# W's mirrored rows by indirect DMA, x in eight pieces, two more pairs' sums on TensorE, and a new order of items, in a two-layer spectral and dense kernel

## The chip, the cores and the metric

The kernel runs on one core of a Trainium2 chip. A core has a matmul engine (TensorE, PE in the profile, with PEld for its weight loads), a vector engine (VectorE, DVE), an activation engine (ScalarE, ACT), a general engine (GpSimd, POOL) and a queue engine (SyncE, SP) that issues most DMAs; ACT and POOL can issue DMAs too. Each engine runs its own list of instructions in order, and the engines wait for each other through semaphores. The metric is the device time of one execution in microseconds (us): lower is better.

## The reference

Two layers, each a spectral filter (A) and a dense block (B), both on a layer-normalised x of 2048 x 448 in bf16, with the same weights in both layers.

```
def _A_ref(x, w_r, w_i):                   # x: (1, 2048, 448)
    X = rfft2(x.astype(float32))           # 2048 x 225
    X = X * (w_r + 1j * w_i)
    return irfft2(X, s=(S, D)).astype(bfloat16)

def _B_ref(x, w1, b1, w2, b2):             # w1: 448 x 1792, w2: 1792 x 448
    h = x @ w1 + b1
    r = where(h > 0, h, 0)
    return (r * r) @ w2 + b2

x = x + _A_ref(_layernorm(x)); x = x + _B_ref(_layernorm(x))
x = x + _A_ref(_layernorm(x)); x = x + _B_ref(_layernorm(x))
```

## The kernel before

The transforms are matmuls with constant matrices. The 2048 rows are split as 16 x 128. Partition p of `xin` holds rows 16p to 16p + 15, so that tile t is row 16p + t of every partition.

- **First transform (A1)**, for each of 16 tiles: statistics of the layer norm (on DVE; on ACT for tiles 1, 3 and 5, `act_stats`, L835), a root on ACT and a reciprocal on DVE, then `first_A` (L859). It scales the 128 x 256 matrix `FA_sb` by the tile's 1/std into `Fs`, on POOL, ACT or DVE, and runs five matmuls of 256 columns with `xin`, with `xr` (the mirrored half of the columns, made by eight copies "XR" of two tiles each) and with the mean. The result is copied from PSUM to `XA`.
- **Transform along D (TD)**, for each of eight pairs p of the 16 components (pair 0 holds components 0 and 8): `stage_TD` (L916), result in `U`.
- **B**: `stage_B` (L933), the transform over the remaining 128 positions by `G_sb`, result in `EF`. A pair's two results E and F are those of the real and of the imaginary component.
- **W**: `stage_W` (L966), on DVE. It forms E - F and E + F with parts exchanged (L978, L979), except where TensorE has made the sums (`V_PAIRS`, in layer 2), then four products with W and four to eight sums, into `Z`. It is called for pair 1, pairs 2 and 3, pairs 4 and 5, pairs 6 and 7, and pair 0.
- **Bi** (`stage_Bi`, L1005), the inverse over the 128 positions, by `H_sb` or `HS_sb`, into `VT`; then `stage_TI` and `stage_AI`, which complete the inverse for tiles of rows and add x; then the second norm and the dense block: `h_part`, `h_pairs`, `o_tile`. `w1_aux` (L784) makes column sums of w1 for the folded norm, 16 matmuls with a block of ones; three DMAs write them to a row block of `W1_sb`.

W has a row for each of 2048 frequencies. Pair p needs rows 16k + p and, mirrored over k, rows 16(127 - k) + 16 - p. Before, the second kind is loaded as it stands into `Wn`, which shares memory with `yT`, and `w_mirror` (L802) turns its partitions round: two matmuls of 224 columns with the exchange matrix `J_sb`, and a copy from PSUM to `Wt`. `Wt` is 32 rows of 224 elements to a partition; `Wp` and `W08` are views of it.

The order of the work is fixed: every instruction (or group on one PSUM tile) is an item with a number, and `ORDER` lists the numbers for each engine. The scheduler (`_Sched.schedule`, L347) takes the head of each list, gives out the eight PSUM banks, and fills gaps of PE that it foresees with matmuls of a block of ones (L1338). A tile's waits are worked out from what it reads and writes. The DMA lists are part of `ORDER`: SP issues its DMAs in the order of its list, and an issue that has to wait holds up all behind it.

Of the kernel before, what the change touches and what calls it, by code (L numbers as in the profile page):

```python
# [6 lines left out]
ALU = mybir.AluOpType  # L7
BF16 = mybir.dt.bfloat16
FP32 = mybir.dt.float32

# [14 lines left out]
V_PAIRS = (1, 2, 3, 4, 5, 6, 7)  # L25
H_PAIRS = tuple(p for p in range(1, 8) if p not in SD_PAIRS)
# [10 lines left out]
def make_constants():  # L37
# [64 lines left out]
    for g, M in enumerate((cl * np.cos(th), cl * np.sin(th))):  # L102
        for r in range(2):
# [4 lines left out]
    return dict(HS=HS, FA=np.concatenate([FA, -FA], 1), FI=np.concatenate([FI, -FI], 1), TD=TD, G=G, H=H, TI=TI, TQ=TQ,  # L108
                J=np.eye(P)[::-1])
# [17 lines left out]
1332 1373 1382 1387 1392 1397 1402 1407 1412 1420 1423 1417 1426 1429""",  # L127
# [142 lines left out]
class _Sched:  # L270

    ENGINES = ("pe", "act", "dve", "pool", "sp")
    NDSEM = {"sp": 20, "pool": 16, "act": 8, "pe": 0, "dve": 0}
    DMA_RATE = 400.0
    TURN = 100.0
    BEGIN = 800.0
    WINDOW = 3413.0  # L280

    def __init__(self):
        self.ops = {e: [] for e in self.ENGINES}
# [1133 lines left out]
```

## Time and profile before

| | |
|---|---|
| time, median of 3 runs | 271.43 us (271.36 to 272.04) |
| the profiled execution's own time | 271.52 us |
| its span, first to last instruction | 269.7 us |
| PE busy | 261.0 us, 97% |
| DVE / ACT / POOL busy | 206.1 / 178.9 / 11.9 us |
| DMA | 16.71 MB, of which 10.85 MB read from HBM and 1.84 MB written |
| granted TensorE clock | 0.999 |

The span is what the profile sees; the time holds some 1.8 us more around it. The profile's slices cut the span in 40 parts of 6.74 us, and a digit is the busy tenths of a slice. A line of the timeline has the start in us, the duration (of a merged run of instructions, from the first start to the last end), the engine, the line of the kernel, the operation, out<-in, and in brackets the idle time before it and what ended it. A line of groups has the count, the busy time and the mean of one in ns, then the idle time before. Matmul ends are modelled; the steps from start to start are what PE took.

### The profile page before, as it was taken

The page shows a single profiled execution, that of the slowest core. Times are in us where ns is not written, and L with a number is a line of the kernel's source. Part 1 is how long each engine was busy: PE and PEld are TensorE (multiplying, and loading weights), DVE is VectorE, ACT ScalarE, POOL GpSimd, SP SyncE. Part 2 cuts the span into 40 slices and gives each one's busy share as a digit, 9 for nine tenths or more (in the row PEclk, how much of TensorE's full clock was granted, in tenths as well). Part 3 has the DMA queues.
Part 4 walks back from the last instruction along what each step waited for, and adds up shares of the span by engine and source line. Part 5 has one row for each costly group of instructions (what it writes and reads, how often), then busy time and mean ns, then how long its engine had stood idle before and what let it go on. Part 6 is the DMA issues. An engine that isn't in the chain of part 4 may idle for free.

```text
span 269.7 us, 5684 instructions
## 1 busy us (share of the span) xinstructions
PE 261.0 (97%) x2084; PEld 161.5 (60%) x2084; DVE 206.1 (76%) x737; ACT 178.9 (66%) x395; POOL 11.9 (4%) x27
## 2 busy tenths in 40 slices
PE   8799998999999999999999999999999999999995
PEld 3587656778545564444557875687754565554454
DVE  3898994999999995198896999599978378440452
ACT  4999978996639578884026795897837887001920
POOL 4840000000000000000000000000000000000000
PEclk9999999999999999999999999999999999999999
DMA  7999322022210232200000000002232200230015
GB/s 259 358 336 384 116 24 43 2 40 41 39 36 1 43 69 39 41 0 2 1 0 2 2 0 1 2 1 43 39 74 41 58 0 0 41 73 0 2 34 187
DMA packets 28566, 16.71 MB, mean 62 GB/s; under 512 B 21838, under 2 KB 27194, under 8 KB 28412
## 3 DMA queue, kind: packets, MB, share of 16 engines
q1 hardware_dynamic: 28108, 15.62, 21.2%
q10 hardware_dynamic: 432, 0.75, 0.7%
q8 instruction: 16, 0.26, 0.4%
q14 instruction: 10, 0.08, 0.1%
HBM read 10.85 MB, written 1.84 MB: 47 GB/s over the span
## 4 chain that ended last, share of the span: by engine, by line
PE 78%; DVE 13%; ACT 5%; DMA 1%; issue 1%; POOL 1%; DVEq 0%
PE ps L661 78%; DVE tmp L715 4%; DVE arena L715 2%; DMA xin<-in_A_x_dram 1%; ACT arena L686 1%; DVE VT L687 1%; DVE x_sb L1227 1%; DVE st L818 1%; ACT tmp L686 1%; DVE xin L715 1%; ACT arena L841 0%; PE ps L1338 0%; ACT L680 0%; ACT arena L840 0%; DVE x_sb L1086 0%
## 5 line engine op out<-in xcount | busy, mean ns | idle before, releaser
L661 PE MATMUL ps<-yT,W_sb 64*128 64x512 bf16 (+1 forms) x770 | 90.5, 346 | 0.0
L661 PE MATMUL ps<-W_sb,arena 128*128 128x448 bf16 (+1 forms) x476 | 87.1, 341 | 0.0
L661 PEld LDWEIGHTS ps<-yT,W_sb 64*128 64x128 bf16 (+1 forms) x770 | 52.7, 95 | 33.2 <-ACT arena L680 2.0
L680 ACT ACTIVATE arena<-ps,b1col 128x512 bf16<-128x512 f32 x84 | 52.5, 689 | 26.5 <-PE ps L661 25.9
L661 PEld LDWEIGHTS ps<-W_sb,arena 128*128 128x128 bf16 x476 | 46.1, 98 | 37.3 <-DVE arena L715 1.3
L715 DVE TENSOR_TENSOR arena<-arena 128x512 bf16<-128x512 bf16 (+1 forms) x140 | 44.6, 367 | 21.7 <-ACT arena L680 21.4
L686 ACT ACTIVATE arena<-ps 128x448 bf16<-128x448 f32 (+1 forms) x40 | 26.1, 751 | 2.8 <-PE ps L661 2.7
L1110 ACT ACTIVATE VT<-x_sb 128x448 bf16<-128x448 bf16 x32 | 18.6, 583 | 12.8 <-DVE x_sb L1086 12.8
L1227 DVE SCALAR_TENSOR_TENSOR x_sb<-ps,arena 128x448 bf16<-128x448 f32 (+1 forms) x26 | 15.0, 582 | 14.5 <-PE ps L661 14.5
L680 ACT ACTIVATE mv<-mv,epst 128x1 f32<-128x1 f32 (+1 forms) x41 | 11.8, 296 | 19.1 <-DVE mv L819 12.0
L680 ACT ACTIVATE arena<-ps 128x256 bf16<-128x256 f32 x56 | 18.2, 400 | 1.4 <-PE ps L661 1.4
L686 ACT ACTIVATE XA<-ps 128x512 bf16<-128x512 f32 x28 | 15.4, 591 | 3.3 <-PE ps L661 3.1
L686 ACT ACTIVATE VT<-ps 128x512 bf16<-128x512 f32 (+1 forms) x26 | 13.5, 612 | 5.3 <-PE ps L661 5.3
L661 PE MATMUL ps<-yT,VT 64*128 64x512 bf16 x42 | 15.8, 376 | 0.0
L686 ACT ACTIVATE tmp<-ps 128x896 bf16<-128x896 f32 (+1 forms) x18 | 14.3, 840 | 1.2 <-PE ps L661 1.2
L661 PE MATMUL ps<-HS_sb,arena 128*128 128x512 bf16 x64 | 14.8, 379 | 0.0
L661 PE MATMUL ps<-arena,G_sb 128*128 128x448 bf16 (+1 forms) x72 | 13.9, 332 | 0.0
L661 PE MATMUL ps<-TD_sb,XA 112*128 112x112 bf16 (+1 forms) x184 | 13.7, 229 | 0.0
L661 PEld LDWEIGHTS ps<-TD_sb,XA 112*128 112x128 bf16 (+1 forms) x184 | 12.2, 98 | 1.9 <-ACT XA L686 0.4
L1086 DVE SCALAR_TENSOR_TENSOR x_sb<-ps,x_sb 128x448 bf16<-128x448 f32 x16 | 9.7, 619 | 3.0 <-PE ps L661 3.0
L1086 DVE SCALAR_TENSOR_TENSOR x_sb<-ps,xin 128x448 bf16<-128x448 f32 x16 | 9.7, 617 | 2.7 <-PE ps L661 2.7
L661 PE MATMUL ps<-TI_sb,VT 112*128 112x112 bf16 (+1 forms) x128 | 10.0, 224 | 1.3 <-ACT VT L686 0.7
(89 smaller groups left out, 314.7 us busy)
## 6 DMA issues: line engine op xcount, KB each, us to landing
out_dram<-x_sb SPq DMA_DIRECT2D x15, 112.0 KB, 1.8
W_sb<-in_B_w_dram SPq DMA_DIRECT2D x1, 1568.0 KB, 10.7
W_sb<-in_B_w_dram SPq DMA_DIRECT2D x1, 1344.0 KB
HS_sb<-c_HS SPq DMA_DIRECT2D x1, 1024.0 KB, 7.3
xin<-in_A_x_dram SPq DMA_DIRECT2D x2, 448.0 KB, 5.9
G_sb<-c_G SPq DMA_DIRECT2D x1, 672.0 KB, 8.8
xin<-in_A_x_dram ACTq DMA_DIRECT2D x1, 448.0 KB, 5.9
yT<-in_A_w_r_dram SPq DMA_DIRECT2D x1, 392.0 KB, 10.9
```

Source lines behind the costliest of these rows:

```text
L661: return sch.add("pe", lambda e: e.matmul(_res(o), lhsT, rhs, start=start, stop=stop, skip_group_check=skip), [lhsT, rhs], [o], cost=cost, ...
L680: sch.add("act", lambda e: e.activation(o, _res(i), func, **kw), rd, [o], cost=c)
L686: op = sch.add(engs[0], lambda e: e.activation(o, _res(i), ACT.Copy) if h[0].eng == "act" else e.tensor_copy(o, _res(i)), [i], [o], cost=c ...
L687: e.tensor_copy(o, _res(i)), [i], [o], cost=c[engs[0]], unit=unit)
L715: sch.add(eng, lambda e: e.tensor_tensor(o, _res(a), b, op), [a, b], [o], cost=_free(o) / rate + 69.0)
L818: small(lambda e, si=si, xi=xi: e.bn_stats(si, xi), [xi], [si], _free(xi) / 0.96 + 69.0)
L1086: small(lambda e, xx=xx, xi=xi, r=r, i=i: e.scalar_tensor_tensor(out=xx, in0=_res(r), scalar=1.0, in1=xi, op0=ALU.mult, op1=ALU.add, accum ...
L1110: sch.add("act", lambda e, i=i, o=o, x=x: e.activation(o, x, ACT.Square, accum_out=sd[:, i, 1:2]), [x], [o, sd[:, i, 1:2]], cost=560.0)
L1227: small(lambda e: e.scalar_tensor_tensor(out=o, in0=_res(i), scalar=r[0] if r else 1.0, in1=xb[:, t, d0:d1], op0=ALU.mult, op1=ALU.add), [ ...
```

## The change

1. **Mirrored rows.** `Wn`, `w_mirror` and its loads go. `Wt` becomes 32 rows of 225 elements, so that a whole row of W is kept and seven of them are one run of 3150 bytes in HBM. Two indirect DMAs on POOL fetch, for each partition, the seven rows that start at the row number in `ix`, a 128 x 1 table of constants that SP loads. The rows that are not mirrored are loaded by SP with k from 7 down to 1. `Wp` is a view that reverses k and skips element 0 of each row, and `W08` and its uses skip it too.
2. **Loads.** x comes in eight pieces of two tiles, the even ones on SP and the odd ones on ACT, `FA_sb` is the second item made and goes on SP. ACT's first instruction is a root (for its table), ahead of its DMAs. The padding of `x_sb` is cleared for tiles 0 to 3 alone, on POOL; block 3 of `W1_sb` is cleared on POOL and for all partitions.
3. **Sums.** In layer 1, pairs 2 and 3 get their E - F and E + F from four matmuls of 448 columns for each result, in place of two, with one more constant `GN_sb`; `stage_W` then leaves out L978 and L979 for them.
4. **Order.** All lists of `ORDER` are new. PE starts with the tiles 3, 2, 0, 4, 1, 5 (before: 0, 2, 3, 1, then one of tiles 8 and 9); `w1_aux` stands between the first transform and TD (before: among the B items); Bi of pair 1 stands ahead of the last TD items. POOL does the memsets, the first gather, four XR copies (tiles 2, 0, 10 and 4 and their neighbours), then scales and copies, with the second gather ahead of the last XR copy and the last three scales. SP issues ix, x 0, x 2, FA, x 4, W1 (three blocks), x 6, W1 (the rest), W08's first part, GN, G, b1, TD, the two row loads, FI, HS, G's pair 0, J, TI, H, the three rows of `w1_aux`, b2, a row of b1, H's pair 0, W08's second part, a row of b1, W2. ACT issues x 1, x 5, x 3, x 7.
5. **Tail.** The last tile of the output is cut at 336 columns and no longer at 224.

```
@@ make_constants @@
+    IX = (16 * (P - 1 - np.arange(P)) + 9)[:, None]
+    GN = -G[:, [p + 1 for p in VB_PAIRS], 0]
@@ _Sched @@
-        dma_free = 3900.0
+        dma_free = self.DMA_FIRST
@@ tiles @@
-        Wn = yT[:].rearrange("p a b c -> p (a b c)")[:, 0:2 * 7 * LW].rearrange("p (r k l) -> p r k l", r=2, k=7)
-        Wt = sb("Wt", [P, 32, LW])
+        Wt = sb("Wt", [P, 32 * (LW + 1)])
+        ix = sb("ix", [P, 1], U32)
...
+        GN_sb = sb("GN_sb", [P, max(len(VB_PAIRS), 1), P])
...
-        Wp = Wt[:, 0:28, :].rearrange("p (q s) l -> p q s l", s=4)
-        W08 = Wt[:, 28:32, :].rearrange("p (q s) l -> p q s l", s=2)
+        Wk = Wt[:, 0:28 * (LW + 1)].rearrange("p (s k l) -> p s k l", s=4, k=7)
+        Wp = Wk[:, :, ::-1, 1:].rearrange("p s k l -> p k s l")
+        W08 = Wt[:, 28 * (LW + 1):].rearrange("p (q s l) -> p q s l", s=2, q=2)
@@ loads @@
-        pieces = ((0, 2), (2, 4), (4, 8), (8, 12), (12, 16))
-        for i, (a, b) in enumerate(pieces):
-            if i == 2:
-                dma("act", FA_sb[:], dc["FA"])
-            dma("act" if i in (1, 3) else "sp", xin[:, a:b, :], x_dram[:, a:b, :])
+        sch.table_deps = [sch.last_write[k] for k in _pages(warm[:, 0:1])][:1]
+        for i in range(8):
+            dma("act" if i % 2 else "sp", xin[:, 2 * i:2 * i + 2, :], x_dram[:, 2 * i:2 * i + 2, :])
+            if i == 0:
+                dma("sp", FA_sb[:], dc["FA"])
+            if i == 5:
+                dma("sp", ix[:], idx)
         memset(ones[:], 1.0, eng="pool")
         sch.warm_deps = [sch.last_write[k] for k in _pages(ones[:])][:1]
+        memset(x_sb[:, 0:4, D:4 * P], 0.0, eng="pool")
...
-        memset(x_sb[:, :, D:4 * P], 0.0, eng="pool")
-        memset(W1_sb[64:128, 3, :], 0.0)
+        def gather(i):
+            o = Wk[:, 3 - 2 * i].rearrange("p k l -> p (k l)")
+            sch.add("pool", lambda e: e.indirect_dma_start(o, None, (A_w_r, A_w_i)[i], bass.IndirectOffsetOnAxis(ix[:], 0)),
+                    [ix[:]], [o], is_dma=True, cost=1500.0, lat=1100.0)
+
+        sch.bias, sch.tag = PR["M"], "M"
+        for i in range(2):
+            gather(i)
+        sch.bias, sch.tag = 0.0, ""
+        memset(W1_sb[:, 3, :], 0.0, eng="pool")
...
+        if VB_PAIRS:
+            dma("sp", GN_sb[:], dc["GN"])
         for i in range(2):
-            dma("sp", Wn[:, i, :, :], w_dram[i][:, 9:16, 1:225])
-        dma("sp", G_sb[:, 2:9], dc["G"][:, 2:9])
-        for i in range(2):
-            dma("sp", Wp[:, :, 2 * i, :], w_dram[i][:, 1:8, 1:225])
+            dma("sp", Wk[:, 2 * i], w_dram[i][:, 7:0:-1, :])
...
-        def w_mirror(p):
-
-            q = _Tile(1)
-            for i in range(2):
-                mm(q[lambda b, i=i: ps[:, b, i * LW:(i + 1) * LW]], J_sb[:], Wn[:, 1 - i, 7 - p, :],
-                   i == 0, i == 1, skip=True)
-            evac(Wp[:, p - 1, 1:4:2, :],
-                 q[lambda b: ps[:, b, 0:2 * LW].rearrange("p (r l) -> p r l", r=2)], EV["M"])
@@ stage_B @@
-        def stage_B(p):
+        def stage_B(p, first):
+            if first and p in VB_PAIRS:
+                i, n = p + 1, GN_sb[:, VB_PAIRS.index(p)]
+                ur, ui = U[:, 2 * p, :], U[:, 2 * p + 1, :]
+                sr, si = (u.rearrange("p (r l) -> p r l", r=2)[:, ::-1] for u in (ur, ui))
+                c, m, s = (G_sb[:, i, k] for k in range(3))
+                for e, t in enumerate((((c, ur), (s, ui), (s, sr), (n, si)), ((m, ur), (c, ui), (c, sr), (s, si)))):
+                    q = _Tile(1)
+                    for k, (g, u) in enumerate(t):
+                        mm(q[lambda b: ps[:, b, 0:2 * LW]], g, u, k == 0, k == 3)
+                    evac(EF[:, 2 * p + e, :], q[lambda b: ps[:, b, 0:2 * LW]])
+                return
@@ stage_W @@
-                if not first and p0 in V_PAIRS:
+                if p0 in (VB_PAIRS if first else V_PAIRS):
                     T[0:2] = E, F
...
-                tt(T[0], X, W08, ALU.mult)
-                tt(T[1], X, W08[:, :, ::-1, :], ALU.mult)
+                tt(T[0], X, W08[:, :, :, 1:], ALU.mult)
+                tt(T[1], X, W08[:, :, ::-1, 1:], ALU.mult)
@@ spectral, ffn @@
+        CUT2 = ((0, 3 * QD), (3 * QD, D)) if HALVES else ((0, D),)
...
-                if first and p > 0:
-                    sch.bias, sch.tag = PR["M"] - PR["step"][L] * n, f"M.{n}"
-                    w_mirror(p)
...
-                    for d0, d1 in (CUT if t == NT - 1 else ((0, D),)):
+                    for d0, d1 in ((CUT2 if last else CUT) if t == NT - 1 else ((0, D),)):
```

with `VB_PAIRS = (2, 3)`.

More of the change, by code (lines that the diff above doesn't have):

```diff
@@ L9 @@
 FP32 = mybir.dt.float32
+U32 = mybir.dt.uint32
 P = 128
@@ L25 @@
 V_PAIRS = (1, 2, 3, 4, 5, 6, 7)
+VB_PAIRS = (2, 3)
 H_PAIRS = tuple(p for p in range(1, 8) if p not in SD_PAIRS)
@@ L277 @@
     DMA_RATE = 400.0
+    DMA_FIRST = 3600.0
     TURN = 100.0
@@ L291, in __init__ @@
         self.warm_deps = []
+        self.table_deps = []
         self.warm_from = 0.0
@@ L318, in add @@
             op.gdeps += [d for d in self.warm_deps if id(d) not in deps]
+        if eng == "act" and not is_dma:
+            op.gdeps += [d for d in self.table_deps if id(d) not in deps]
         op.deps = [d for d in deps.values() if d is not op and not (d.eng == "pe" and eng == "pe")]
@@ L638, in bass_interleave_layers__spectral_gfnet__dense_activation_squared_relu__prompt_kernel @@
                 sem[(e, True, j)] = es.enter_context(nc.semaphore(f"s_{e}_dma{j}"))
+        loads = []
         def dma(eng, o, i, transpose=False, after=()):
+            if not sch.tag or sch.tag[0] == "L":
+                sch.tag = f"L.{len(loads)}"
+                loads.append(o)
             reads = ([i] if i.tensor.name in onchip else []) + list(after)
@@ L773, in bass_interleave_layers__spectral_gfnet__dense_activation_squared_relu__prompt_kernel @@
         for i in range(2):
-            dma("sp", W08[:, :, i, :], w_dram[i][:, 0:9:8, 1:225])
+            dma("sp", W08[:, :, i, :], w_dram[i][:, 0:9:8, :])
         dma("sp", TI_sb[:], dc["TI"])
@@ L1255, in spectral @@
                 stage_TD(p, first)
-                if first and p > 0:
-                    sch.bias, sch.tag = PR["M"] - PR["step"][L] * n, f"M.{n}"
-                    w_mirror(p)
                 rank("B", n)
-                stage_B(p)
+                stage_B(p, first)
                 rank("W", n)
```

20 lines of the change are left out of this document (11 added, 9 removed), and 95 rows, old and new, of the table ORDER.

## The prediction

> **What bounds the kernel now.** I read the busy shares and the slices first, to see which engine is full and where it is not.
>
> ```profile
> span 269.7 us, 5684 instructions
> ...
> PE 261.0 (97%) x2084; PEld 161.5 (60%) x2084; DVE 206.1 (76%) x737; ACT 178.9 (66%) x395; POOL 11.9 (4%) x27
> ...
> ACT  4999978996639578884026795897837887001920
> ...
> GB/s 259 358 336 384 116 24 43 2 40 41 39 36 1 43 69 39 41 0 2 1 0 2 2 0 1 2 1 43 39 74 41 58 0 0 41 73 0 2 34 187
> ...
> PE 78%; DVE 13%; ACT 5%; DMA 1%; issue 1%; POOL 1%; DVEq 0%
> ```
>
> TensorE (PE) is busy for 97% of the span, and the chain that ended last is 78% PE. Busy matmuls are modelled, so I checked PE's spacing below: it issues at its steady pitch almost everywhere. Time can therefore come only from the start, from PE's few waits, and from matmuls that are taken away or added. The slices (6.74 us each) show that ACT is nearly as full early on: 9, 9, 9, 7 and 8 after the first. The windows of the stages that the diff touches give the amounts.
>
> ```profile
> 9.00:18.30 9.30, 9.07 (x80) 7.53 (x81) 9.07 (x43) 9.26 (x27) 7.46 (x16) 1.00 1.09 339
> ...
> 19.20:44.80 25.60, 24.75 (x188) 16.59 (x188) 22.93 (x53) 22.82 (x40) 0.00 (x0) 1.00 0.54 162
> 147.40:170.30 22.90, 22.54 (x221) 15.53 (x220) 21.19 (x45) 17.36 (x31) 0.00 (x0) 1.00 0.00 1
> ```
>
> The columns are PE, weight loads, DVE, ACT, POOL. The first row is the first transform (16 tiles of five matmuls): ACT is busy 9.26 of 9.30 us and DVE 9.07, so an earlier PE start alone does not shorten it. The second is layer 1's spectral part, where PE has 24.75 of 25.60 us, DVE 22.93 and ACT 22.82. The third is the same part of layer 2.
>
> Then the timeline of the start, all engines.
>
> ```profile
> 4.69 1.06 POOL L687 COPY VT<-xin 128x448 bf16<-128x448 bf16 x2 [2.86 <-DMA xin<-in_A_x_dram]
> ...
> 5.90 1.28 ACT L680 ACT_TABLE_LOAD   x1
> ...
> 7.20 0.48 ACT L680 ACTIVATE mv<-mv,epst 128x1 f32<-128x1 f32 x2
> ...
> 8.37 0.93 POOL L698 TENSOR_SCALAR Fs<-FA_sb,rstd 128x256 bf16<-128x256 bf16 x2 [0.71 <-DMA FA_sb<-c_FA]
> ...
> 8.99 0.27 PE L661 MATMUL ps<-Fs,xin 128*128 128x256 bf16 x1 [1.73 <-POOL Fs L698]
> ```
>
> Before 8.99 PE runs only filler. The path to 8.99 is: x lands (by 4.69), ACT's sums, a second table load of 1.28 us, the square roots (7.20), the reciprocals, then POOL's scaled transform matrix Fs, which was ready to start 0.71 us earlier but waited for FA_sb.
>
> PE's own timeline from there has every number for the terms that follow.
>
> ```profile
> 18.24 0.27 PE L661 MATMUL ps<-Fs,m 128*128 128x256 bf16 x1
> 18.35 0.93 PE L661 MATMUL ps<-yT,J_sb 128*128 128x224 bf16 x8
> 19.25 1.69 PE L661 MATMUL ps<-TD_sb,XA 128*128 128x224 bf16 x16
> 20.78 0.92 PE L661 MATMUL ps<-arena,G_sb 128*128 128x448 bf16 x4
> 21.53 0.93 PE L661 MATMUL ps<-TD_sb,XA 128*128 128x224 bf16 x8
> ...
> 28.39 0.35 PE L661 MATMUL ps<-yT,J_sb 128*128 128x224 bf16 x2
> 28.59 0.93 PE L661 MATMUL ps<-TD_sb,XA 128*128 128x224 bf16 x8
> 29.35 0.35 PE L661 MATMUL ps<-yT,J_sb 128*128 128x224 bf16 x2
> 29.66 1.68 PE L661 MATMUL ps<-arena,G_sb 128*128 128x224 bf16 x12
> 31.18 0.35 PE L661 MATMUL ps<-yT,J_sb 128*128 128x224 bf16 x2
> 31.71 0.94 PE L661 MATMUL ps<-W_sb,ones 128*32 128x448 bf16 x16 [0.18 <-ACT arena L686]
> ...
> 44.81 0.45 PE L661 MATMUL ps<-TI_sb,VT 112*128 112x224 bf16 x3 [0.68 <-ACT VT L686]
> ```
>
> **The change, part by part.** *Mirrored rows without J matmuls.* Fourteen matmuls go, in four places. Eight take 18.35 to 19.25 (0.90 us); the pairs take 28.39 to 28.59 (0.20), 29.35 to 29.66 (0.31) and 31.18 to 31.71 (0.53, with the 0.18 us wait for ACT). All of it is on PE's line: 0.90 + 0.20 + 0.31 + 0.53 = 1.94 us less. Their seven copies out of PSUM leave too, four on ACT and three on DVE:
>
> ```profile
> L715 DVE TENSOR_TENSOR tmp<-arena 128x896 bf16<-128x896 bf16 (+1 forms) x8 | 4.3, 562 | 0.5 <-ACT arena L686 0.5
> ...
> L686 ACT ACTIVATE Wt<-ps 128x448 bf16<-128x448 f32 x4 | 2.3, 563 | 0.2 <-PE ps L661 0.2
> ...
> L687 DVE CAST Wt<-ps 128x448 bf16<-128x448 f32 x3 | 1.7, 617 | 0.0
> ```
>
> That is 2.3 us of ACT and 1.7 of DVE. It is not counted as a gain of its own, since the two waits that it caused on PE (in the 0.31 and the 0.53) are in the 1.94 already. The first eight matmuls also gave ACT and DVE time to empty the last transform tiles before TD; that cover is taken over by w1_aux, whose 16 matmuls (0.94 us by their row at 31.71) move to just this place. So the aux move costs nothing; without it TD would wait up to 0.9 us for those copies.
>
> *Sums of pairs 2 and 3 on TensorE.* Four matmuls more for each pair, eight of 448 columns. Four take 20.78 to 21.53, 0.19 us each: 8 x 0.188 = 1.50 us more on PE. DVE loses two subtract/add instructions of 896 elements (0.56 us each in the first row above), which is on the path only where DVE is last; I take nothing for it. PE's price would be hidden only if PE had waited there, and in 20 to 28 us it does not.
>
> *Start.* Two waits go: the table load of 1.28 us (ACT now loads the root's table before any data) and the 0.71 us for FA_sb (now third or fourth on SP's queue). Together 1.99 us, the upper bound. Against it stand three delays. ACT's queue holds x pieces 1, 5, 3, 7 behind that same table load and a 0.19 us root, so they are issued up to 1.47 us later than now (0.73). SP issues ix first, so piece 0 comes one issue later (three issues take 1.35 us in the row below: 0.45). And PE now begins with tile 3, which lies in piece 1, while POOL makes four mirrored copies (4 x 0.53 from the row 4.69) before its first Fs. POOL's first copy thus starts at 4.69 + 0.5 to 4.69 + 1.47, so 5.2 to 6.2; plus 2.1 for copies, 0.5 for Fs and 0.1 to PE gives 7.9 to 8.9. I take 8.3, 0.7 us earlier than 8.99, as the issue may pass the table load or not. The whole transform then shifts by this 0.7 only: by the window above ACT and DVE are full, and what moves between engines cancels (ACT two Fs more and one copy less, DVE the reverse, POOL one Fs less and the gathers more). PE alone would need 80 matmuls of 0.109 us (18.24 to 18.35), 8.7 us, against 9.36 now.
>
> By the Trainium skill's page ScalarE: Activation LUTs (What ACT_TABLE_LOAD costs) a switch of tables takes about 2.66 us, because a drain of 1.38 us follows the load. The trace differs: the load took 1.28 us and the next ACT work started 0.02 us behind it; by the page the upper bound would be 3.4 us, not 1.99.
>
> *The two gathers.* No DMA issued by POOL is in this trace. The nearest rows are issues on SP:
>
> ```profile
> 0.73 1.35 SPq L653 DMA_DIRECT2D xin<-in_A_x_dram  x3
> ...
> 5.44 3.88 SPq L653 DMA_DIRECT2D J_sb<-c_J  x1
> ...
> 35.97 0.67 SPq L653 DMA_DIRECT2D W_sb<-yT  x1
> ...
> 39.09 0.56 SPq L653 DMA_DIRECT2D W_sb<-yT  x1
> ...
> 57.35 1.33 SPq L648 DMA_TRANSPOSE yT<-x_sb  x1
> ```
>
> The lower bound is 0.45 us of POOL's time (a plain issue), the upper 3.88 (J_sb's 32 KB, held back by the loads queued ahead of it). I take 1.3, as the transposing DMA's 1.33: also an issue that spells out many small moves, with nothing queued ahead. The first gather stands behind the memsets, which end near 3.8 (0.73 plus about 3.0 us for 3200 elements at the 0.95 us per 1024 shown below), and waits for ix, SP's first issue: should a 512-byte load land as late as the first x does now (4.69), the gather would end at 6.0, else at 5.1. Both are within piece 1's 5.2 to 6.2: nothing. The second stands ahead of POOL's last copy and last three Fs. From a first Fs at 7.7, POOL has 11 Fs of 0.48, four copies of 0.56 and 1.3: it ends at 16.5, while PE at 8.3 + 8.7 + today's 0.64 us of waits ends at 17.65. Nothing again, with about 0.6 us to spare.
>
> ```profile
> L698 POOL TENSOR_SCALAR Fs<-FA_sb,rstd 128x256 bf16<-128x256 bf16 x12 | 5.7, 478 | 1.7 <-DMA FA_sb<-c_FA 0.7 <-PE ps L661 0.7 <-DVE mv L819 0.2
> L687 POOL COPY VT<-xin 128x448 bf16<-128x448 bf16 x8 | 4.4, 557 | 3.3 <-DMA xin<-in_A_x_dram 3.3
> ...
> L728 POOL MEMSET x_sb<- 128x1024 bf16 x1 | 1.0, 951 | 0.0
> ```
>
> *Loads.* TD_sb now stands behind x, FA, W1, one W08 part, GN and G_sb: with itself 4.5 MB by the shapes. On POOL's queue up to one and a half gathers of 0.4 MB pass beside it, and I allow 0.3 for b1in, which goes in 2-byte pieces: 5.4 MB. The GB/s row (6.74 us a slice) has moved 1.75 + 2.41 = 4.16 MB by 13.5 us and goes on at 336, so TD arrives near 17.2 plus under 1 us, against TD's need at 18.5. The W rows (1.0 MB more, near 20.2) are needed by DVE at about 22.4 (its first product starts at 23.04, rival 2). Covered, by about 1 us; if not, DVE's W products are late, and with them layer 1's Bi matmuls. The three copies of aux's rows also stand earlier on SP, each waiting for the one before (35.97 to 39.09, 3.1 us), with H_sb[0:2], W08's second part and W2 behind them: from about 19.5 that is to 29. Pair 0, which uses the first two, ends layer 1 (before 44.81) and W2 follows it: covered by several us.
>
> *Tail.* The last tile is cut 336/112 and not 224/224:
>
> ```profile
> 266.88 0.39 DVE L1227 SCALAR_TENSOR_TENSOR x_sb<-ps,arena 128x224 bf16<-128x224 f32 x1 [0.95 <-PE ps L661]
> ```
>
> Half the elements of this 0.39 us instruction: about 0.1 us less, as some 0.2 us of it is fixed. The matmuls in sum are the same.
>
> *Order elsewhere.* Layer 2 and the dense parts hold the same matmuls in another order; I take 0, with 0.5 us either way.
>
> **Sum.** -1.94 + 1.50 - 0.70 - 0.10 = -1.24 us. The profiled execution took 271.52 us (span 269.7), so 270.28; it stood 0.09 above the median of 271.43, so I forecast 270.2. Its own range, from a start gain of 0 to 1.99 and the 0.5 of the order: 268.4 to 271.4.
>
> **Rivals.** (1) *POOL becomes the bound* (slower). If a gather holds POOL for g, the first ends at 3.8 + g and the second adds g - 1.3 ahead of the last Fs, less the 0.6 us spare. For: POOL alone makes all mirrored copies and 11 of 16 Fs. Against: 1.33 us as the nearest row. At g = 3 the first costs 1.1 (6.8 against 5.7) and the second 1.1: 272.4; at 3.88, 274.2. It is slower from about g = 2.9.
>
> (2) *DVE's W products lose their double rate* (slower). In Wt rows are now 225 elements and the products start at element 1, so every other row starts 2 bytes off a 4-byte word.
>
> ```profile
> 23.04 1.29 DVE L715 TENSOR_TENSOR tmp<-tmp,Wt 128x448 bf16<-128x448 bf16 x4
> ...
> 26.48 0.62 DVE L715 TENSOR_TENSOR tmp<-arena 128x896 bf16<-128x896 bf16 x1
> ```
>
> ```profile
> 130.66 0.44 DVE L715 TENSOR_TENSOR xin<-x_sb 128x224 bf16<-128x224 bf16 x2
> ```
>
> Here a product of 448 takes 0.32 us and an 896-element instruction 0.54 to the next (26.48 to 27.02), 0.5 ns an element; a copy from PSUM takes 0.617 us for 448 (above), about 1.05 ns an element beyond its start. At that rate a product of 896 costs 0.46 us more. There are 14 of 896 and 4 of 448 a layer: 7.4 us. In layer 2 DVE is busy 21.19 of 22.90, so some 5.7 shows, and in layer 1, after 2.8 us relief and 2.7 of idle, 1.9: 277.8. For: DVE is that full, and no row shows a forward operand of this kind. Against: the nearest row (130.66) reads x_sb backwards from element 447, so from 2 bytes off a word, and its two instructions of 224 still take 0.44 us, the double rate. The Trainium skill disagrees with itself here: VectorE: DVE Perf Modes (Mode 2×_1P) asks for 4-byte alignment, while Vector Engine (DVE) Microarchitecture Reference (5.1) reports that alignment made no difference on trn2. By the one, this rival is the forecast; by the other, nothing happens. No run here shows which holds.
>
> (3) *The early part is hidden*: TD or the W rows land late, or piece 1 lands at 6.2 and the first transform ends at 18.35 as now. Then J's 1.94 pays for the 1.50 and for a wait of some 0.4 to 1: 271.4.
>
> (4) *More than counted*: ACT 2.3 us and DVE 2.8 us lighter also shorten the 0.68 us wait before 44.81 and the start gains its 1.99: 268.3.
>
> **How the numbers follow.** Forecast 0.48, rival 1 0.12, rival 2 0.07, rival 3 0.21, rival 4 0.12. A measurement tells 0.3%, 0.81 us, from no change: faster is below 270.6. The forecast lies 0.4 us beyond that line, so I give it 0.41 faster and 0.07 same; rival 4 is faster, rival 3 mostly same (0.17) and else slower, rivals 1 and 2 slower. Faster 0.53, same 0.24, slower 0.23. The range 268.2 to 273.2 leaves out rival 2, the upper half of rival 1 and a little below.
>
> **What would show it.** First real matmul near 8.3 and end of the transform near 17.6; no second table load; no J matmuls before the flips; TD right behind aux without a wait for DMA; POOL's gathers at about 1.3 us; W products of 896 still at 0.56 us; TI of layer 1 starting near 43.6 for 44.81. A POOL release ahead of PE's last transform tiles speaks for rival 1, products near 1.0 us for rival 2, a DMA release of TD or of the W products for rival 3. Wrong altogether if layer 2, which keeps its matmuls, changes by more than 1 us.

## The result, and the profile after

The changed kernel took 272.90 us (median of 15 runs, 272.34 to 274.90), beside 271.67 us for the kernel before in runs on the same chip (15 runs, 271.36 to 272.87). The ratio is 1.0045, with a 95% interval of 1.0025 to 1.0066: slower by 0.45%, where the forecast was 270.2 us and faster. The profiled execution took 272.98 us, with a span of 271.2 us where it was 269.7. The time lies above the 271.4 of rival 3, which named the mechanism, and on the other side from the forecast.

First the page of the changed kernel: busy times, bytes moved by slice (6.8 us each) and the chain that ended last, by engine; then two pieces of that chain (start, duration, what).

```profile
span 271.2 us, 5675 instructions
...
PE 260.9 (96%) x2079; PEld 164.6 (61%) x2079; DVE 202.7 (75%) x733; ACT 174.9 (64%) x390; POOL 14.5 (5%) x29
...
GB/s 225 366 261 298 74 277 21 2 0 75 45 36 2 39 71 39 41 0 2 1 0 2 0 2 1 2 1 41 40 70 81 37 2 0 2 105 57 36 34 85
...
PE 71%; DVE 12%; ACT 7%; DMA 5%; SPq 2%; issue 2%; ACTq 0%; DVEq 0%
```

```profile
7.16 13.54 DMA TD_sb<-c_TD
20.83 24.29 PE ps L677 x172
```

PE's busy time is as before (261.0), so the loss is not work that it does but time in which it waits. The chain has lost 7 points of PE, and DMAs now are 5% of it where they were 1%: one piece of 13.54 us, the load of TD_sb, from its issue to its landing at 20.70, right before PE goes on at 20.83. The third slice moved 261 GB/s where the kernel before moved 336 and the prediction counted on 336.

Next the timeline of PE through the early part (start, duration, instructions, and in brackets the idle time with what ended it).

```profile
7.69 0.27 PE L677 MATMUL ps<-Fs,xin 128*128 128x256 bf16 x1 [0.75 <-POOL Fs L714]
...
14.35 0.27 PE L677 MATMUL ps<-Fs,m 128*128 128x256 bf16 x1
15.72 0.27 PE L677 MATMUL ps<-Fs,xin 128*128 128x256 bf16 x1 [1.09 <-ACT Fs L713]
...
18.33 0.94 PE L677 MATMUL ps<-W_sb,ones 128*32 128x448 bf16 x16
20.83 2.08 PE L677 MATMUL ps<-TD_sb,XA 128*128 128x224 bf16 x20 [1.55 <-DMA TD_sb<-c_TD]
...
45.03 0.26 PE L677 MATMUL ps<-TI_sb,VT 112*128 112x224 bf16 x1
```

PE's first real matmul comes 1.30 us earlier than before (7.69 for 8.99). ACT's timeline (ACTq is its queue of issues) shows why: its loads of x were issued while its table load ran, and the first x was in by 3.95.

```profile
0.72 1.28 ACT L696 ACT_TABLE_LOAD   x1 [0.72 <-PEq L1429]
0.89 1.35 ACTq L669 DMA_DIRECT2D xin<-in_A_x_dram  x3
...
3.95 0.58 ACT L858 ACTIVATE arena<-xin 128x448 bf16<-128x448 bf16 x1 [1.72 <-DMA xin<-in_A_x_dram]
```

In the timeline of PE, by the end of the transform the gain is gone, lost in the gap between 14.35 and 15.72: DVE's statistics of a tile had waited 1.63 us for x, until 14.34, and the Fs that PE needs comes behind them. Then aux runs from 18.33, and TD cannot start until 20.83: PE waited 1.55 us for the load of TD_sb, and TD starts 1.58 us later than before (19.25). From there to the start of TI, layer 1's spectral part takes 45.03 - 20.83 = 24.20 us. Before it took 43.87 - 19.25 = 24.62, as TI's first matmul in PE's timeline before shows:

```profile
43.87 0.26 PE L661 MATMUL ps<-TI_sb,VT 112*128 112x224 bf16 x1
```

So the spans differ by +1.58 (start of TD), -0.42 (TD to TI) and +0.28 (TI to the end: 271.18 - 45.03 for 269.74 - 43.87), together +1.44. The last of the three is not a property of the new order: the same stretch took 225.7 us in run e1, 225.8 in g4 and 225.9 in f3, which keep the new order, where it took 225.87 before.

Why TD_sb was late is seen on SP's queue. The timeline of the queue shows when each load was issued and how long the issue itself took; the DMA view gives for each load its size and the time from issue to landing; the waits of SP name what held an issue back (us in total, times, longest).

```profile
6.01 0.45 SPq L669 DMA_DIRECT2D G_sb<-c_G  x1
6.50 0.62 SPq L669 DMA_DIRECT2D b1in<-in_B_b_dram  x1
7.16 8.14 SPq L669 DMA_DIRECT2D TD_sb<-c_TD  x1
...
19.66 0.38 SPq L669 DMA_DIRECT2D Wt<-in_A_w_r_dram  x1
...
23.79 0.44 SPq L669 DMA_DIRECT2D H_sb<-c_H  x1
```

```profile
G_sb<-c_G SPq DMA_DIRECT2D x1, 672.0 KB, 12.2
...
H_sb<-c_H SPq DMA_DIRECT2D x1, 384.0 KB, 5.6
...
TD_sb<-c_TD SPq DMA_DIRECT2D x1, 224.0 KB, 13.5
...
b1in<-in_B_b_dram SPq DMA_DIRECT2D x1, 3.5 KB, 13.6
```

```profile
SPq L669 <- DMA Wt<-in_A_w_i_dram,ix: 2.5, 1, 2.5
```

G_sb landed at 6.01 + 12.2 = 18.2, b1in at 6.50 + 13.6 = 20.1 and TD_sb at 7.16 + 13.5 = 20.7. Between G_sb and TD_sb lie 224 KB of TD_sb and the 3.5 KB of b1in, in 1792 pieces of 2 bytes. The last row is a wait that the prediction did not have: SP stood 2.5 us, from 17.17 to 19.66, until POOL's second gather had landed, before it issued the load of Wt_r. All that follows on the queue stood with it, H_sb's second part among it (landed 23.79 + 5.6 = 29.4).

Two rivals fell by the same trace. The gathers, with what POOL did around the second, and DVE's W products, as groups of one shape with their mean:

```profile
3.77 1.16 POOL L774 DMA_INDIRECT Wt<-in_A_w_r_dram,ix  x1 [0.17 <-issue]
...
12.63 1.03 POOL L774 DMA_INDIRECT Wt<-in_A_w_i_dram,ix  x1 [0.16 <-issue]
14.37 0.55 POOL L703 COPY VT<-xin 128x448 bf16<-128x448 bf16 x1 [0.70 <-DMA xin<-in_A_x_dram]
```

```profile
L731 DVE TENSOR_TENSOR tmp<-arena,Wt 128x896 bf16<-128x896 bf16 x20 | 11.6, 623 | 0.2
```

```profile
L715 DVE TENSOR_TENSOR tmp<-arena,Wt 128x896 bf16<-128x896 bf16 x16 | 9.2, 619 | 0.1
```

A gather held POOL for 1.16 and 1.03 us (1.3 taken), so rival 1, which needed 2.9, did not happen; POOL's own wait of 0.70 was for x's piece 6, which stands behind the first W1 load on SP's queue. A product of 896 took 623 ns where it took 619, so rival 2, the loss of the double rate, did not happen either: here the Trainium skill's page Vector Engine (DVE) Microarchitecture Reference (5.1) holds, by which alignment made no difference, and VectorE: DVE Perf Modes (Mode 2×_1P) does not.

### The profile page after: what moved, and what is told of

The parts are those of the page before. It is cut to its first block, busy times and chain, and to the rows that moved or that the text cites. A ratio compares the mean times of both kernels' runs of the same rounds, so it can differ in the third digit from the quotient of the medians.

```text
span 271.2 us, 5675 instructions
## 1 busy us (share of the span) xinstructions
PE 260.9 (96%) x2079; PEld 164.6 (61%) x2079; DVE 202.7 (75%) x733; ACT 174.9 (64%) x390; POOL 14.5 (5%) x29
## 4 chain that ended last, share of the span: by engine, by line
PE 71%; DVE 12%; ACT 7%; DMA 5%; SPq 2%; issue 2%; ACTq 0%; DVEq 0%
PE ps L677 71%; DMA TD_sb<-c_TD 5%; SPq L669 2%; DVE arena L731 2%; ACT VT L1139 2%; ACT tmp L702 2%; DVE x_sb L1256 2%; DVE tmp L731 2%; DVE st L836 1%; ACT VT L702 1%; DVE x_sb L1115 1%; DVE xin L731 1%; ACT arena L696 1%; ACT mv L696 1%; PE ps L1365 0%
## 5 line engine op out<-in xcount | busy, mean ns | idle before, releaser
L677 PE MATMUL ps<-W_sb,arena 128*128 128x448 bf16 (+3 forms) x476 | 86.6, 342 | 0.0
L677 PEld LDWEIGHTS ps<-yT,W_sb 64*128 64x128 bf16 (+1 forms) x770 | 56.1, 95 | 29.0 <-ACT arena L696 2.2
L696 ACT ACTIVATE arena<-ps,b1col 128x512 bf16<-128x512 f32 x84 | 51.8, 692 | 18.5 <-PE ps L677 18.3
L1139 ACT ACTIVATE VT<-x_sb 128x448 bf16<-128x448 bf16 x32 | 18.5, 584 | 13.7 <-DVE x_sb L1115 13.6
L696 ACT ACTIVATE mv<-mv,epst 128x1 f32<-128x1 f32 (+1 forms) x41 | 11.5, 292 | 23.1 <-DVE mv L837 18.5
L1256 DVE SCALAR_TENSOR_TENSOR x_sb<-ps,arena 128x448 bf16<-128x448 f32 (+3 forms) x26 | 15.1, 584 | 14.6 <-PE ps L677 14.5
L702 ACT ACTIVATE VT<-ps 128x512 bf16<-128x512 f32 (+1 forms) x28 | 13.6, 571 | 4.3 <-PE ps L677 4.3
L677 PE MATMUL ps<-arena,G_sb 128*128 128x448 bf16 (+1 forms) x78 | 15.7, 333 | 0.0
L702 ACT ACTIVATE XA<-ps 128x512 bf16<-128x512 f32 x27 | 14.6, 592 | 1.6 <-PE ps L677 1.6
L731 DVE TENSOR_TENSOR tmp<-arena,Wt 128x896 bf16<-128x896 bf16 (+1 forms) x24 | 13.0, 584 | 0.2
## 6 DMA issues: line engine op xcount, KB each, us to landing
G_sb<-c_G SPq DMA_DIRECT2D x1, 672.0 KB, 12.2
```

Source lines behind the costliest of these rows:

```text
L677: return sch.add("pe", lambda e: e.matmul(_res(o), lhsT, rhs, start=start, stop=stop, skip_group_check=skip), [lhsT, rhs], [o], cost=cost, ...
L696: sch.add("act", lambda e: e.activation(o, _res(i), func, **kw), rd, [o], cost=c)
L702: op = sch.add(engs[0], lambda e: e.activation(o, _res(i), ACT.Copy) if h[0].eng == "act" else e.tensor_copy(o, _res(i)), [i], [o], cost=c ...
L731: sch.add(eng, lambda e: e.tensor_tensor(o, _res(a), b, op), [a, b], [o], cost=_free(o) / rate + 69.0)
L1139: sch.add("act", lambda e, i=i, o=o, x=x: e.activation(o, x, ACT.Square, accum_out=sd[:, i, 1:2]), [x], [o, sd[:, i, 1:2]], cost=560.0)
L1256: small(lambda e: e.scalar_tensor_tensor(out=o, in0=_res(i), scalar=r[0] if r else 1.0, in1=xb[:, t, d0:d1], op0=ALU.mult, op1=ALU.add), [ ...
```

## The experiments

Each kernel is compared with the kernel before on the same chip; times are medians. In the order lists, SP's items are 11 x's piece 6, 44 and 45 W1, 37 and 38 the two parts of W08, 30 GN_sb, 29 G_sb, 42 b1in, 28 TD_sb, 32 and 31 the W rows of i and r, 40 FI_sb, 34 HS_sb, 35 G_sb's first part, 27 J_sb, 39 TI_sb, 33 H_sb's second part.

**e1: TD_sb first.**

```diff
-45 37 30 29 42 28 32 31 40 34 35 27 39 33
+45 37 28 30 29 42 32 31 40 34 35 27 39 33
```

> The changed kernel with one load moved on SP's queue: TD_sb ahead of GN_sb, G_sb and b1in, nothing else. Theory A (the loss sits in the wait for TD_sb: aux has issued all by 18.92 and TD starts at 20.83, when TD_sb's load, landed 20.69, is in): TD_sb passes 0.75 MB and b1in, some 4 us of queue, lands near 16.5, TD starts at 19.25 or before with no wait for a DMA, and the kernel takes 1.4 to 1.6 us less than the changed one's 272.9: 271.3 to 271.5, ratio to the kernel before 0.999. Rival B (the W rows, landed 22.04 and 23.98, bind next, since DVE's products cannot start before them): half of it at most comes back, 272.2, and DVE's first products wait for a DMA. Rival C (the wait is covered later, the loss comes from the order of the later items): 272.9, ratio 1.0045.

Measured: 272.98 us, ratio 1.0058 (1.0034 to 1.0082): no gain at all, so theory A as written fell. The trace shows that the wait did go. PE's timeline of this run:

```profile
17.24 0.94 PE L677 MATMUL ps<-W_sb,ones 128*32 128x448 bf16 x16
18.20 2.08 PE L677 MATMUL ps<-TD_sb,XA 128*128 128x224 bf16 x20
...
30.96 0.60 PE L677 MATMUL ps<-H_sb,arena 128*128 128x256 bf16 x4 [2.71 <-DMA H_sb<-c_H]
...
45.27 0.26 PE L677 MATMUL ps<-TI_sb,VT 112*128 112x224 bf16 x1
```

TD starts right behind aux at 18.20, 2.63 us earlier than in the changed kernel. At 28.09 all of it is lost again: PE waits 2.71 us for H_sb's second part, issued behind Wt_r and five more loads. SP stood twice on the way: 3.4 us for the first gather, ahead of the load of Wt_i, and 4.5 for the second, ahead of that of Wt_r. In the changed kernel the first of these waits is hidden, as TD_sb's issue held the queue until 15.30, and the first gather landed at 3.77 + 7.6 = 11.4. TI starts at 45.27, even a little later. In the changed kernel the same matmuls came at 30.72, when H_sb had been in for 1.3 us: the wait for TD_sb had covered this one.

**e2: b1in late.** DVE's cast of b1in (43) is moved later as well.

```diff
-45 37 30 29 42 28 32 31 40
+45 37 30 29 28 32 31 42 40
```

> The changed kernel with b1in's load moved behind the two W row loads, and with DVE's cast of it moved later to match. Theory A2 (it is b1in, 1792 pieces of 2 bytes, and not the megabytes ahead of TD_sb, that made TD_sb late: G_sb landed at 18.19 and b1in at 20.11): TD_sb lands near 18.8, TD starts near 19.3, the W rows land 1.9 us earlier as well, and the kernel takes 271.3 to 271.5. Rival (volume: the queue moves the same bytes whichever way, b1in's small ones among them): TD_sb still lands after 20.4 and the time is 272.9.

Measured: 273.43 us, ratio 1.0082 (1.0055 to 1.0108). The DMA view of this run, with TD_sb issued at 6.42 and G_sb at 5.95:

```profile
G_sb<-c_G SPq DMA_DIRECT2D x1, 672.0 KB, 10.6
...
TD_sb<-c_TD SPq DMA_DIRECT2D x1, 224.0 KB, 10.8
```

TD_sb landed at 17.2, 0.65 us behind G_sb, where it was 2.5 us behind with b1in between. In the four traces with b1in ahead of TD_sb at the same place (the changed kernel, e3, e4 and g4) it landed at 20.2 to 20.7. Theory A2 is right on the cause, and took it too small: the 3.5 KB of b1in cost TD_sb 3.0 to 3.5 us, where A2 had 1.9. The time did not follow: TD started at 18.18, and the wait at 28 was there as in e1 (2.61 us).

**e3: x's piece 6 first.**

```diff
-10 3 6 4 8 44 11 45
+10 3 6 4 8 11 44 45
```

> The changed kernel with x's piece 6 ahead of the first W1 load on SP's queue, nothing else. Both theories expect PE's wait of 1.26 us at 14.35 to go and the transform to end near 17.2 where it ended at 18.24. Theory A (TD_sb's landing at 20.69 sets the start of the rest): TD still starts at 20.8 and the time stays within 0.3 us of 272.9. Rival (what PE loses in the transform is lost for good): 271.8.

Measured: 274.06 us, ratio 1.0086 (1.0058 to 1.0115). The wait at 14.35 is gone and aux starts at 16.74, but TD still at 20.64. That theory A foresaw, but not that the time would rise. Five of the six executions, the profiled one among them, ran at a granted clock of 0.994 or less over the whole span (273.57 to 275.50 us); the one at 1.00 took 272.84, as the changed kernel. PE's timeline and its windows (busy time, granted clock, share and GB/s of the DMA engines):

```profile
16.74 0.94 PE L677 MATMUL ps<-W_sb,ones 128*32 128x448 bf16 x16
20.64 3.19 PE L677 MATMUL ps<-TD_sb,XA 128*128 128x224 bf16 x20 [2.96 <-DMA TD_sb<-c_TD]
```

```profile
20.60:23.00 2.40, 2.36 (x17) 0.67 0.89 217
23.00:25.00 2.00, 2.00 (x10) 0.54 0.91 291
```

PE has now been idle for 2.96 us, and what follows runs at a granted clock of 0.67 and then 0.54: the first 20 TD matmuls take 3.19 us where they took 2.08. In this execution the wait cost more than its own length.

**e4: the late items in their old order.** All items from layer 2's spectral part on stand in the order of the kernel before, on every engine.

> The changed kernel with all items from layer 2's spectral part on in the order that they have in the kernel before; what lies ahead of it is unchanged. In the changed kernel the stretch from layer 2's TD to the first matmul of its dense part took 29.46 us where it took 29.18, and from there to the last matmul 90.87 where it took 90.25. Theory D (the new order costs these 0.28 and 0.62 us): 272.0. Rival (they follow from how the engines reach this stretch, not from the order): 272.9 as before.

Measured: 272.61 us, ratio 1.0046 (1.0029 to 1.0062), and the spread of the runs is wider than the 0.3 us in question. Inconclusive by itself; g2 below asks again where the early part is steady.

**f1: TD_sb and H_sb first.**

```diff
-45 37 30 29 42 28 32 31 40 34 35 27 39 33 163
+45 37 28 30 29 42 32 33 31 40 34 35 27 39 163
```

> Run e1 (TD_sb first) with one more load moved on SP's queue: H_sb's second part ahead of the Wt_r rows, and so ahead of FI_sb, HS_sb, G_sb's first part, J_sb and TI_sb as well. In run e1 TD started at 18.20 and the 2.6 us won there were lost again at 28.09, where PE waited 2.71 us for H_sb, landed 30.83. Theory E (two late loads, one behind the other: TD_sb, and H_sb, whose landing covers up whatever is won ahead of it): H_sb lands before 25, no wait at 28, TI of layer 1 starts near 42.6 (45.27 in e1), and the kernel takes 270.2 to 270.5, ratio 0.995. Rival F (a third wall stands behind it, DVE's W products, which waited 0.83 for Wt_r in e1 and now wait longer, or HS_sb): at most 1 us of it comes back, 271.9.

Measured: 271.89 us, ratio 0.9995 (0.9977 to 1.0014). The 2.71 us wait at 28 is gone and 1.1 us of time with it, which is between the two expectations; rival F has the rest. DVE's timeline of this run, and PE's:

```profile
24.96 0.70 DVE L731 TENSOR_TENSOR tmp<-tmp,Wt 128x448 bf16<-128x448 bf16 x2 [0.83 <-DMA Wt<-in_A_w_r_dram]
```

```profile
35.98 6.62 PE L677 MATMUL ps<-HS_sb,arena 128*128 128x512 bf16 x28 [0.23 <-DVE arena L731]
```

Wt_r, moved behind H_sb, landed at 24.94, and DVE's products waited for it. PE then waited for DVE's products instead (0.40 us beyond its pitch at 35.6, and 0.29 within the stretch that starts at 35.98). The transform, too, lost its 1.2 us at 14.36 again in this execution.

**f2: a gap in Wt**, on top of e1's order.

```diff
-        Wt = sb("Wt", [P, 32 * (LW + 1)])
+        Wt = sb("Wt", [P, 32 * (LW + 1) + 4])
...
-        Wk = Wt[:, 0:28 * (LW + 1)].rearrange("p (s k l) -> p s k l", s=4, k=7)
+        Wk = Wt[:, 0:28 * (LW + 1) + 4].rearrange("p (s x) -> p s x", s=4)[:, :, 0:7 * (LW + 1)]\
+            .rearrange("p s (k l) -> p s k l", k=7)
```

> Run e1 (TD_sb first) with a gap of one element behind each 7 x 225 block of W rows in Wt. A block is 1575 elements of 2 bytes, so that two neighbours share one 4-byte word, and the schedule, which tracks words, makes the SP load of Wt_r wait for POOL's second gather (SP stood from 17.17 to 19.66 and issued when the gather had landed at 19.64). With the gap nothing is shared and that wait is not there. Theory G (the shared word holds back everything behind Wt_r on SP's queue, H_sb among them): Wt_r is issued near 17 and H_sb lands some 2.5 us earlier, near 28.3; PE's wait of 2.71 us at 28.09 falls to under 0.5, and the kernel takes 270.4 to 270.9. Rival (the queue moves no more bytes per us, so HS_sb's 1 MB, ahead of H_sb, lands no earlier): 272.5 to 272.9.

Measured: 271.35 us, ratio 0.9984 (0.9969 to 0.9998): 1.6 us less than e1, by one unused element a block. SP's queue and PE's timeline of this run:

```profile
15.71 1.21 SPq L669 DMA_DIRECT2D Wt<-in_A_w_r_dram  x1
...
22.80 0.42 SPq L669 DMA_DIRECT2D H_sb<-c_H  x1
```

```profile
28.84 0.60 PE L677 MATMUL ps<-H_sb,arena 128*128 128x256 bf16 x4 [0.53 <-DVE arena L731]
```

Wt_r is issued at 15.71, as soon as the queue takes it, and H_sb at 22.80 (23.79 in the changed kernel). PE's wait at 28 fell from 2.71 to 0.53 us (the row puts it down to DVE's products; H_sb, too, had only landed at 28.7, behind HS_sb's 1 MB). Theory G holds for SP's wait, and nearly for PE's (under 0.5 expected); the time came out 0.5 us above its range.

**f3: all loads in the order of need**, with f2's gap.

```diff
-10 3 6 4 8 44 11 45 37 30 29 42 28 32 31 40 34 35 27 39 33 163
+10 3 6 4 8 11 44 45 28 30 29 32 31 33 40 34 35 27 39 37 42 163
```

> The changed kernel with all of its loads in the order of their need: x's piece 6 ahead of W1, TD_sb right behind W1, then GN_sb, G_sb, the W rows, H_sb's second part, and only then W08's first part and b1in (DVE's cast of it later too); with the gap of run f2. Theory E: transform, aux and TD follow each other without a wait, TD starts near 17.9, no wait at 28, and the kernel takes 269.7 to 270.2, ratio 0.994. Rival F (DVE's W products or HS_sb bind behind it): 271 or more.

Measured: 270.09 us (270.07 to 270.53), ratio 0.9939 (0.9917 to 0.9961): faster than both kernels, as theory E had it. PE's timeline of this run:

```profile
16.77 0.94 PE L677 MATMUL ps<-W_sb,ones 128*32 128x448 bf16 x16
17.73 2.08 PE L677 MATMUL ps<-TD_sb,XA 128*128 128x224 bf16 x20
...
27.62 0.60 PE L677 MATMUL ps<-H_sb,arena 128*128 128x256 bf16 x4
...
34.05 0.59 PE L1366 MATMUL ps<-ones 128*128 128x512 bf16 x2
...
42.36 0.26 PE L677 MATMUL ps<-TI_sb,VT 112*128 112x224 bf16 x1
```

Transform, aux and TD follow each other, and nothing waits at 28. TI starts 1.51 us earlier than before. From TD to TI it takes 24.63 us: 0.43 more than in the changed kernel, which are the two filler matmuls at 34.05 (L1366) that the schedule puts in where it expects PE to wait. All five runs with the gap have them, and none without it. They seem to be lost time: the sums for which PE's HS_sb matmuls waited in g3 (DVE ended them at 34.36 there, PE went on at 34.42) were done at 33.44 in f3. A run of f3 without the fillers was not made.

**f4 and g1: the eight matmuls of the sums left out**, in f1 and in f3.

```diff
-                    for k, (g, u) in enumerate(t):
-                        mm(q[lambda b: ps[:, b, 0:2 * LW]], g, u, k == 0, k == 3)
+                    for k, (g, u) in enumerate(t[:2]):
+                        mm(q[lambda b: ps[:, b, 0:2 * LW]], g, u, k == 0, k == 1)
```

> Run f1 with the eight matmuls for the sums of layer 1's pairs 2 and 3 left out: each of the four accumulations takes two matmuls where it takes four, so E and F enter the W products without being summed. It measures what the 1.50 us of these matmuls are worth where no load is late. If TensorE bounds this part: 1.5 us less than run f1 (TI of layer 1 starts 1.5 earlier). If the evacuations or DVE's W products bound it: the same time as f1 within 0.3 us.

> Run f3 with the eight matmuls for the sums of layer 1's pairs 2 and 3 left out, as in run f4. In f4 a late Wt_r held DVE up and PE waited for its products, so the price of these matmuls could not be read; in f3 no load is late. If TensorE bounds layer 1's spectral part, as the prediction's +1.50 has it: 268.6, and TI of layer 1 starts near 40.9 (42.36 in f3). If DVE's products set the pace, so that PE's extra 1.50 us fills time in which it would have waited: 269.8 to 270.1, with waits of PE for DVE of 1 us or more between 18 and 42.

Measured: f4 272.68 us, ratio 1.0028 (1.0011 to 1.0044), not less than f1 but 0.8 us more; g1 270.24 us (269.95 to 270.46), ratio 0.9953 (0.9940 to 0.9967), no less than f3. In f4 the late Wt_r set the pace: PE waited 1.15 us for DVE's products at 35.8, so that TI started at 44.13, beside 44.27 in f1; later it lost 0.80 at 190.8, waiting for a transposing DMA. In g1, PE's timeline shows where 1.50 us went:

```profile
23.57 1.71 PE L677 MATMUL ps<-TD_sb,XA 128*128 128x224 bf16 x16 [0.17 <-ACT arena L702]
...
33.49 6.56 PE L677 MATMUL ps<-HS_sb,arena 128*128 128x512 bf16 x28
...
41.72 0.26 PE L677 MATMUL ps<-TI_sb,VT 112*128 112x224 bf16 x1
```

```profile
188.12 4.10 PE L677 MATMUL ps<-yT,W_sb 128*128 128x256 bf16 x36 [0.33 <-DMA yT<-x_sb]
```

TI starts at 41.72, 0.64 us earlier than in f3 and not 1.50: PE now has small waits for ACT and DVE (0.17 at 23.4, a stretch of HS_sb matmuls of 6.56 us for 6.21, and others). Of the 0.64, some 0.5 is lost at 188, where PE waits for a transposing DMA, and the rest is below what the runs can tell. So neither expectation held alone: 0.64 of the 1.50 is on the path in layer 1, and none of it in the time. Why the transposing DMA at 188 comes no earlier was not tried.

**g2: f3 with the late items in their old order.**

> Run f3 with the items from layer 2's spectral part on in the order of the kernel before, as in run e4. In e4's trace the stretch from layer 2's TD to the dense part took 29.19 us for 29.46, the dense part to the last matmul 90.25 for 90.87, and the end after it 2.99 for 2.50. If these 0.40 us belong to the order: 269.7. If not: 270.1 as f3.

Measured: 270.10 us (270.06 to 270.12), the same as f3's 270.09. The new order of layer 2 and of the dense parts costs nothing and brings nothing in sum.

**g3: f3 without the gap; g4: the gap alone in the changed kernel.** The edits are f2's gap, taken out of f3 and put into the changed kernel.

> Run f3 without the gap in Wt: Wt_r's load waits again for POOL's second gather, landed near 20, and H_sb, FI_sb, HS_sb and all behind it on SP's queue with it. Theory G: Wt_r lands near 24 (21.89 in f3), DVE's second pair of W products waits about 1.3 us for it, and H_sb lands near 25, still ahead of its need at 27: 271.0 to 271.5, as f1 shows for such a wait. Rival (the order alone made f3's gain): 270.1.

> The changed kernel with the gap in Wt and nothing else. Theory E (two late loads in series: TD_sb, behind b1in, and those that wait for the second gather; each covers the other): TD_sb still lands near 20.6 and TD starts there, so the time stays at 272.7 to 273.0 although SP's wait from 17.2 to 19.7 is gone. Rival (the shared word is the whole loss): 271.4.

Measured: g3 270.77 us (270.51 to 271.00), ratio 0.9965 (0.9950 to 0.9980); g4 272.64 us (272.35 to 272.79), ratio 1.0041 (1.0027 to 1.0055). The gap alone brings 0.3 us at most, while on top of e1 it brought 1.6 and in f3 it brings 0.7. In g3 DVE waited 0.90 us for Wt_r at 22.6, as expected in kind, though less of it reached the end. SP there stood 5.1 us for the first gather and 8.2 for the second: each of the two loads of W rows shares a word with the block of one gather, so the gap unties two pairs, not one.

The four kernels with and without TD_sb first, with and without the gap, make the table that settles the early part:

| | Wt_r waits for the gather | gap, no wait |
|---|---|---|
| TD_sb behind G_sb and b1in | 272.90, ratio 1.0045 (changed kernel) | 272.64, ratio 1.0041 (g4) |
| TD_sb first | 272.98, ratio 1.0058 (e1) | 271.35, ratio 0.9984 (f2) |

Either repair alone is worth nothing to 0.3 us, both together 1.55. Some of the 0.3 and of the 1.55 is clock: 4 of 15 executions of the changed kernel and 4 of 12 of e1 ran at 0.994, and none of g4 and f2. By the executions at 1.00 alone the medians are 272.67, 272.64, 272.85 and 271.35, so that either repair brings nothing and both together 1.3. Two late loads stood one behind the other, and each covered the other.

## Why the prediction was wrong

The step that failed is *Loads*, at its words "Covered, by about 1 us". It had TD_sb in before 18.2, ahead of TD's need at 18.5; TD_sb landed at 20.7 and TD started at 20.83. These 2.3 us are nearly all of the 2.5 between the forecast gain (1.24) and the measured loss (1.23). One thing made TD_sb late, and two more made a second load late behind it.

*b1in.* "I allow 0.3 for b1in" was too little, by ten times: with b1in moved away TD_sb landed at 17.2 (e2), the step's own figure, and with b1in ahead of it 3.0 to 3.5 us later. A row of the kernel before bore on it. There b1in was issued at 37.35, right behind W08's part of r, into a nearly empty queue:

```profile
Wt<-in_A_w_r_dram SPq DMA_DIRECT2D x1, 112.0 KB, 2.6
...
b1in<-in_B_b_dram SPq DMA_DIRECT2D x1, 3.5 KB, 3.6
```

3.5 KB took a microsecond longer to land than 112 KB. The allowance was in effect made by bytes, which cannot explain that; that the price goes by the 1792 pieces is the likely reading, but no run varied their number.

*The rate.* The step carried 336 GB/s on from the slices before; the third slice moved 261. This is not a second cause but b1in seen once more: from 16 to 18 us the changed kernel moved 170 GB/s and e2, with b1in moved back, 363; in f3, where b1in stands behind all of these loads, the third slice moved 330. At that rate the step's sum holds.

*A wait not seen.* The step gave the W rows 20.2, by bytes alone. They landed at 22.0 (i) and 24.0 (r). SP's wait for the second gather (2.5 us) is not what made them late, as without it, in g4, they landed at 21.7 and 23.8; what it held back is H_sb's second part, which came in at 30.9 in e1 and, without the wait, at 28.7 in f2. The cause of the wait is in the rows of 225: a block of 7 x 225 elements of 2 bytes ends inside a 4-byte word, the next block begins in it, and the schedule tracks words. f2, g3 and g4 show it by the gap.

*A load not priced.* H_sb's second part, moved behind HS_sb, FI_sb, J_sb and TI_sb and behind that wait, is not in the step, which priced only H_sb's first two. It was hidden in the changed kernel and became the wall in e1.

The rival that named this was rival 3 ("TD or the W rows land late"), at 0.21, with a wait "of some 0.4 to 1". The wait was 1.55 us and TD was late by 1.58 against before, and the matmuls won between cover only 0.42 of it: the mechanism was there and its size was taken too small. The range reached to 273.2 and held the time.

The other terms, by their own steps:

- *Start*, -0.70: the first matmul gained 1.30, as ACT's issues passed its table load, which the prediction had left open. But "the whole transform then shifts by this 0.7" failed: PE stood 1.26 us at 14.35 for Fs of a tile of x's piece 6. With piece 6 ahead of W1 (e3) that wait went; it was also small in e1 and e4 (0.3 at most) and there again in f1, so it varies from one execution to the next as long as piece 6 stands behind W1. With piece 6 ahead (f3) the whole transform does shift: aux starts at 16.77, where the J matmuls started at 18.35, and TD 1.52 us earlier than before. The term was too small by half. One figure under it was read too large: the 0.71 us ahead of Fs is POOL's idle time, but the reciprocal that Fs needs ended only at 7.71 + 0.16 = 7.87, so that FA_sb cost 0.50 of it.
- *J matmuls and sums*, -1.94 + 1.50 = -0.44: TD to TI measured -0.42 in the changed kernel. (Eight of the J matmuls, 0.90 us, never lay in this stretch, and aux, 0.87 from start to start, left it; the two cancel, as the prediction had it.) As a sum of matmuls on a PE that never waits it was right. That "PE's price would be hidden only if PE had waited there" was right as a rule, but with the loads in order PE is close to waiting: taking the 1.50 away brought 0.64 there (g1), so DVE and ACT are nearly as full as PE.
- *Gathers* and *W products*: as predicted, nothing on the path. That holds for POOL's time; the landing of the second gather, through SP's wait, was on it.
- *Tail*, -0.10: the last evacuation took 0.27 for 0.39 us; nothing larger was seen, and 0.1 us is below what the runs can tell. *Order elsewhere*, 0: as predicted (g2 against f3).

f3 came out at 270.09, near the forecast of 270.2, but that is luck and not its sum: its gain of 1.5 us is the start's alone, where the forecast had 0.70 of the start and 0.44 of the matmuls. The matmuls' 0.42 went into the two fillers.

## What to carry to other kernels

Two late loads in series show only the first of them: when a repaired wait brings nothing, look for the next load on the same queue before dropping the theory, and price every load that a moved item now stands in front of. A load of many tiny pieces needs a row of its own for that, since its bytes say nothing. A layout whose blocks end inside a tracked word ties two transfers together that share no data; a gap of one element unties them. A gain at the start of a stage that is fed by transfers is a gain only if the loads behind it move up as well.

## What the runs showed of the hardware

- A wait of PE can cost more than its length. After 2.96 us idle (e3) the granted clock was 0.67 and 0.54 in the next 4.4 us. After 2.37 us idle (e4's profiled execution) it fell as well, as these windows show:

```profile
20.60:23.00 2.40, 2.35 (x18) 0.72 0.80 193
23.00:25.00 2.00, 2.00 (x9) 0.50 0.94 270
```

  After 1.55 us (the changed kernel), 2.23 (g4), 2.61 (e2) and 2.71 us (e1) the profiled executions stayed at 1.00. So the clock goes to about half, and the length of the wait alone does not decide. The Trainium skill's page TensorE: Matmul & The Clock Gate (Part 1) describes a gate that halves the clock after an idle window of about 3.4 us which runs freely, not from the start of the wait. The runs agree on the half; both waits that were followed by it are shorter than the window that the page gives. What counts as idle, and whether the phase of a window decides, was not tried.
- Executions with a granted clock of 0.994 or less over the whole span came only in kernels whose profile has a wait of PE of over 1.2 us: 15 of 66 of the kernel before (1.73 us ahead of 8.99), 4 of 15 of the changed kernel and 15 of 36 of e1 to e4. Of g4 (2.23 us) there were none of 5, and of the other runs, with waits of 1.15 us at most, none of 62.
- One issue on SP held its queue for 8.14 us (TD_sb's at 7.16), with some 4 MB by the shapes issued ahead of it on SP and ACT; all later issues stood behind it. In f3 it was H_sb's issue at 7.80 that held the queue, for 8.57 us.
- ACT issued loads during its own table load (0.89, in 0.72 to 2.00).
